# A decode block with its gradients on one core: attention by batch instead of by head group, and VectorE 32-bit transposes instead of TensorE transposes

## The chip, the core and the metric

The kernel runs on 1 core of one Trainium2 chip. The metric is the device time of one execution in microseconds (us). The kernel before took 311.61 us in the median of 3 runs (310.44 to 313.74). One further execution was recorded with the hardware profiler; every row of a profile below is from that one.

Engines: PE is TensorE (PEld its weight loads), DVE is VectorE, ACT is ScalarE, POOL is GpSimd, SP is SyncE. SP, ACT and POOL can each issue DMAs, each into a queue of its own (q1, q10 and q0 in the profile); the 16 DMA engines serve all three.

## The reference

One decode step of a block with attention and a feed-forward network (FFN) side by side, and the gradients of all its inputs:

```python
xn  = layernorm(x)                                   # x: [4, 1, 512], bf16
q   = xn @ wq                                        # 32 heads of 128
k,v = last 1024 of 4096 rows of the caches [4, 8, 4096, 128], each kv-head for 4 heads
p   = softmax(q k^T / sqrt(128));  o = p v
out = x + (o @ wo) + (gelu(xn @ w_gate) * (xn @ w_up)) @ w_down    # F = 1792
# and, for grad_out, the gradients of x, k_cache, v_cache, wq, wo, w_gate, w_up, w_down
```

The outputs are `out` and `dx` (tiny), `dk` and `dv` of the whole caches (33.6 MB each, of which the first 3072 of 4096 rows are zeros), `dwq` and `dwo` (4.2 MB each) and the three FFN weight gradients (1.8 MB each). So 81 MB are written and some 31 MB read. Each weight gradient is an outer product over only 4 batches. What takes work is that K, V and every weight are needed in two orientations, one as they lie in memory, and one transposed.

## The kernel before

**Stages.** Constants and the layer norm come first. Then comes the FFN, forward and backward. Then a loop over `t`, the NT = 4 groups of GP = 2 kv-heads (8 heads), each for all 4 batches: `pre` (query rows `qs` and `do` = the gradient that reaches each head's output, through `wo`), `masks`, `scores(t, 0)` (S, from K), `softmax`, `scores(t, 1)` (dP, from V), `softmax_d`, `odq` (rows of `o` and `dq`), `fin` (contributions to `out` and `dx`). The two sums over groups gather in `acc`; a chain of operations on rows finishes `out` and `dx` (lines 652 to 681).

**Transposes.** All are made by PE, as a matmul with the identity into a bf16 PSUM tile of 128x1024 that DVE copies out (`evac(..., half=True)`, line 92): K and V blocks `T_ps` (line 306), `wo` (258), `wq` (471), `w_down` (546), `w_gate` and `w_up` (619).

**Scores.** All four batches and eight heads of a group share one PSUM tile: 128 partitions are 4 quarters of the 1024 keys by 32 rows (batch, head). Four matmuls of 256 columns (line 311), one per quarter, use 32 columns of the array each, at different `tile_position`s.

**Gradient pieces.** A piece of `dv` or `dk` (line 406) is one matmul of 512 columns over 32 rows and one evacuation into a staging tile of 1 MB; eight pieces fill it, and POOL stores it. `dwo`, `dwq` and the FFN's weight gradients are made in pieces in the same way. Pieces aren't emitted where they are defined. They go to a list `bg`, and `tick(n)` emits the next n of them between other steps. `evac` gives each float32 evacuation to ACT or DVE by a running balance of estimated costs (lines 83 to 92).

**Order of issue.** Tile schedules the engines' instructions itself, except those of SP, which keep the written order. SP issues: the rows of `x` and `grad_out`, `w_gate`, `w_up`, `w_down`, `wo` and `wq` of group 0, K and V of group 0 (two tiles each), `wo` and `wq` of group 1, the first K and V tile of group 1, and then the zeros: 32 DMAs of 1.5 MB (line 233), each waiting for the one two before it. All later loads are issued by ACT: K and V (line 213) from rings of three tiles of 1 MB each, `wo` and `wq` (206, 208) of the group after next from rings of two. All results are stored by POOL (line 96), except the two small ones.

**Rows in memory.** A K or V tile has contiguous runs of 2 KB, `wo` and `w_down` runs of 1 KB, `wq` 2 KB, `w_gate` and `w_up` 3.5 KB, zeros 6 KB.

Of the kernel before, what the change touches and what calls it, by code (L numbers as in the profile page):

```python
# [13 lines left out]
BF16 = mybir.dt.bfloat16  # L14
P = 128
# [3 lines left out]
def kernel(  # L19
# [34 lines left out]
    ND = D // P  # L54
    NF = F // P
    J = W // P
    GP = 2
    NT = G // GP
    HG = GP * rep
    RG = B * HG  # L60
    NQ = P // RG
    WQ = W // NQ
    JQ = J // NQ
    NS = B * GP
    CW = HG * Dh
    assert Sq == 1 and Dh == P and D == 512 and F % P == 0 and RG == 32 and JQ * NQ == J and WQ == JQ * P
    scale = float(Dh) ** -0.5
    eps = 1e-5

    const = ctx.enter_context(tc.tile_pool(name="const", bufs=1))  # L70
    kvp = ctx.enter_context(tc.tile_pool(name="kvp", bufs=3))
    wres = ctx.enter_context(tc.tile_pool(name="wres", bufs=2))
    attw = ctx.enter_context(tc.tile_pool(name="attw", bufs=2))
    tsb = ctx.enter_context(tc.tile_pool(name="tsb", bufs=5))
    outp = ctx.enter_context(tc.tile_pool(name="outp", bufs=3))
    ps_w = ctx.enter_context(tc.tile_pool(name="ps_w", bufs=4, space=bass.MemoryType.PSUM))
    ps_a = ctx.enter_context(tc.tile_pool(name="ps_a", bufs=1, space=bass.MemoryType.PSUM))
    ps_x = ctx.enter_context(tc.tile_pool(name="ps_x", bufs=1, space=bass.MemoryType.PSUM))
# [4 lines left out]
    def evac(out, in_, n, half=False, eng=None):  # L83

        eng = "dve" if half else eng
        ca, cd = (190 + n) / 1.2, (120 + (n / 2 if half else n)) / 0.96
        if eng is None:
            eng = "act" if load["act"] + ca <= load["dve"] + cd else "dve"
        load[eng] += ca if eng == "act" else cd
        if eng == "act":  # L90
            return nc.scalar.copy(out=out, in_=in_)  # L91
        return nc.vector.tensor_copy(out=out, in_=in_)  # L92

# [7 lines left out]


    RB = P // B
    x_b = const.tile([P, D], BF16, name="x_b")
    dy_b = const.tile([P, D], BF16, name="dy_b")
    for dst, src in ((x_b, A_x), (dy_b, grad_out)):
        nc.sync.dma_start(out=dst[:], in_=bass.AP(tensor=src.tensor, offset=src.offset,
                                                  ap=[[D, B], [0, RB], [1, D]]))
# [8 lines left out]
    msk_i = const.tile([P, rep], FP32, name="msk_i")  # L117
    nc.vector.reduce_sum(out=msk_i[:], in_=ident_f[:].rearrange("p (b r) -> p r b", b=B)[:, 0:rep, :], axis=AX.X)


    rsum = const.tile([P, NQ, RG], FP32, name="rsum")
    nc.gpsimd.memset(rsum[:], 1.0)

    msk_f = const.tile([P, GP, B], FP32, name="msk_f")
    nc.gpsimd.memset(msk_f[:], 1.0)
    for q in range(NQ):
        rs = slice(q * RG, (q + 1) * RG)
        nc.gpsimd.affine_select(out=rsum[rs], in_=rsum[rs], pattern=[[0, NQ], [-1, RG]],
                                compare_op=ALU.is_equal, fill=0.0, base=0, channel_multiplier=1)
        nc.gpsimd.affine_select(out=msk_f[rs], in_=msk_f[rs], pattern=[[-rep, GP], [-HG, B]],  # L130
                                compare_op=ALU.is_ge, fill=0.0, base=0, channel_multiplier=1)
        nc.gpsimd.affine_select(out=msk_f[rs], in_=msk_f[rs], pattern=[[rep, GP], [HG, B]],
                                compare_op=ALU.is_ge, fill=0.0, base=rep - 1, channel_multiplier=-1)
    msk = const.tile([P, GP, B], BF16, name="msk")
    nc.vector.tensor_copy(out=msk[:], in_=msk_f[:])
# [4 lines left out]

    qm_all, dom_all = [], []
    for i in range(2):
        for lst, nm in ((qm_all, "qm"), (dom_all, "dom")):
            t_ = const.tile([P, NS, RG + rep], BF16, name=f"{nm}{i}")
            nc.gpsimd.memset(t_[:], 0.0)
            lst.append(t_)


    acc = const.tile([P, 2, ND, B], FP32, name="acc")
    nc.vector.memset(acc[:], 0.0)  # L150

    def acc_add(o, ps):
        nc.vector.tensor_tensor(out=acc[:, o], in0=ps, in1=acc[:, o], op=ALU.add)

    def acc_sum(o, terms):

        ps = ps_w.tile([P, ND, B], FP32, name="acc_ps", tag="w")
        for c in range(ND):
            for k, (lf, rhs) in enumerate(terms):
                nc.tensor.matmul(ps[:, c, :], lhsT=lf(c), rhs=rhs, start=(k == 0), stop=(k == len(terms) - 1))  # L160
        acc_add(o, ps[:])


    od_ps = ps_a.tile([P, 2, GP, Dh], FP32, name="od_ps")
    nc.vector.memset(od_ps[:], 0.0)
# [11 lines left out]
    xn_f = const.tile([P, D], FP32, name="xn_f")  # L177
    nc.vector.tensor_scalar(out=xn_f[:], in0=x_b[:], scalar1=mv[:, 0:1], scalar2=rstd[:, 0:1],
                            op0=ALU.subtract, op1=ALU.mult)
    xn_b = const.tile([P, D], BF16, name="xn_b")  # L180
    nc.vector.tensor_copy(out=xn_b[:], in_=xn_f[:])

    xnT = const.tile([P, ND, B], BF16, name="xnT")
    dyT = const.tile([P, ND, B], BF16, name="dyT")
    for src, dstT in ((dy_b, dyT), (xn_b, xnT)):
        tps = ps_x.tile([P, ND, P], BF16, name="tps", tag="x")
        for c in range(ND):
            nc.tensor.transpose(tps[:, c, :], src[:, c * P:(c + 1) * P], ident[:])
        nc.vector.tensor_copy(out=dstT[:], in_=tps[:].rearrange("p c (b r) -> p c b r", b=B)[:, :, :, 0])


    xnm = const.tile([P, rep, D], BF16, name="xnm")
    dym = const.tile([P, rep, D], BF16, name="dym")
    for src, dst in ((dy_b, dym), (xn_b, xnm)):
        for i in range(rep):
            nc.vector.tensor_scalar(out=dst[:, i, :], in0=src[:], scalar1=msk_i[:, i:i + 1], scalar2=None,
                                    op0=ALU.mult)


    wo_v = A_wo.rearrange("(t h p) n -> t p h n", p=P, h=HG)  # L200
    wq_v = A_wq.rearrange("(c p) (t j) -> t p c j", p=P, j=CW)
    wo_t, wq_t, k_t, v_t = {}, {}, {}, {}

    def load_w(t, eng):
        wo_t[t] = wres.tile([P, HG, D], BF16, name="wo_sb", tag="wo")
        eng.dma_start(out=wo_t[t][:], in_=wo_v[t])
        wq_t[t] = wres.tile([P, ND, CW], BF16, name="wq_sb", tag="wq")
        eng.dma_start(out=wq_t[t][:], in_=wq_v[t])  # L208

    def load_kv(t, k, g, eng):  # L210
        d_, src, nm = ((k_t, A_k_cache, "kb"), (v_t, A_v_cache, "vb"))[k]
        tl = kvp.tile([P, B, J, Dh], BF16, name=nm, tag=nm)
        eng.dma_start(out=tl[:].rearrange("p b j d -> p b (j d)"),  # L213
                      in_=src[:, t * GP + g, K0:Sk, :].rearrange("b (m j) d -> m b (j d)", j=J))
        d_[(t, g)] = tl

    def load_next(t, k):

        if t + 1 < NT:
            load_kv(t + 1, k, 1, nc.scalar)  # L220
        if t + 2 < NT:
            load_kv(t + 2, k, 0, nc.scalar)


    ZG = 2
    zlist = [(og, b, g) for b in range(B) for g in range(0, G, ZG) for og in (out_2, out_3)]

    def zeros():

        zsrc = bass.AP(tensor=ztile.tensor, offset=ztile.offset, ap=[list(ztile[:].ap[0]), [0, ZG], [1, ZW]])  # L230
        done = []
        for og, b, g in zlist:
# [8 lines left out]
    bg = deque()  # L241

    def tick(n):
        for _ in range(min(n, len(bg))):
            bg.popleft()()


    st = {}

    def pre(t):  # L250

        wo_sb, wq_sb = wo_t[t], wq_t[t]
        dq_ps = ps_x.tile([P, 2, HG, B], FP32, name="doq_ps", tag="x")
        for h2 in range(HG // 2):
            wT_ps = ps_w.tile([P, 2, ND, P], BF16, name="woT_ps", tag="w")
            for i in range(2):
                for c in range(ND):
                    nc.tensor.transpose(wT_ps[:, i, c, :], wo_sb[:, 2 * h2 + i, c * P:(c + 1) * P], ident[:])  # L258
            woT = tsb.tile([P, 2, ND, P], BF16, name="woT", tag="wT")
            evac(woT[:], wT_ps[:], 1024, half=True)  # L260
            for i in range(2):
                for c in range(ND):
                    nc.tensor.matmul(dq_ps[:, 0, 2 * h2 + i, :], lhsT=woT[:, i, c, :], rhs=dyT[:, c, :],
                                     start=(c == 0), stop=(c == ND - 1))
            tick(2)
        for h in range(HG):
            for c in range(ND):
                nc.tensor.matmul(dq_ps[:, 1, h, :], lhsT=wq_sb[:, c, h * Dh:(h + 1) * Dh], rhs=xnT[:, c, :],
                                 start=(c == 0), stop=(c == ND - 1))
# [27 lines left out]
    def scores(t, k):  # L297
# [4 lines left out]
        for g in range(GP):  # L302
            for b in range(B):
                T_ps = ps_w.tile([P, J, P], BF16, name="T_ps", tag="w")
                for j in range(J):
                    nc.tensor.transpose(T_ps[:, j, :], blks[(t, g)][:, b, j, :], ident[:])  # L306
# [405 lines left out]
```

## Time and profile before

| | |
|---|---|
| median of 3 runs | 311.61 us (310.44 to 313.74) |
| span of the profiled execution, first to last instruction | 311.7 us |
| bytes moved by DMA | 112.38 MB, 34405 packets |
| mean granted PE clock | 0.738 of full |
| busy: PE, DVE, ACT, POOL | 224.1, 146.3, 113.4, 51.3 us |
| queue q1 (SP) | 66.59 MB in 18136 packets |
| queue q0 (POOL) | 30.67 MB in 7808 packets |
| queue q10 (ACT) | 14.69 MB in 8432 packets |
| first and last zeros issued | 38.9 and 256.5 us |

The profile gives a span and no other time for its execution. The page cuts the span into 40 slices of 7.8 us; a digit there is the busy share in tenths. In the groups of instructions, the first two numbers behind the bar are the busy time of the group in us and the mean of one in ns; what follows the second bar is the idle time of that engine just before them, and what ended most of it. The chain of waits is followed back from the last instruction, at each step to whatever released it. ACTq, SPq and POOLq in it are those engines' sequencers issuing DMAs.

### The profile page before, as it was taken

To read this page: it belongs to the slowest core of one execution; us is meant where nothing else is said; L and a number is where in the kernel's file an instruction comes from. 1 tells how busy PE (TensorE), PEld (TensorE's weight loads), DVE (VectorE), ACT (ScalarE), POOL (GpSimd) and SP (SyncE) were. 2 spreads that over 40 slices of the span, in tenths; PEclk is the share of its full clock that TensorE was granted. 3 is DMA by queue.
4 is the path that set the end of the run, shared out by engine and by line. 5 is a ranking of instruction groups with operands and counts; after the bars stand their busy time and mean duration, and the time that the engine had idled before them with its cause. 6 is when DMAs were issued, how large, how long until landed. Compare 5 with 4: busy or idle time off the path is not lost.

```text
span 311.7 us, 6831 instructions
## 1 busy us (share of the span) xinstructions
PE 224.1 (72%) x2950; PEld 144.7 (46%) x2956; DVE 146.3 (47%) x304; ACT 113.4 (36%) x217; POOL 51.3 (16%) x76
## 2 busy tenths in 40 slices
PE   1269986936988379779648069969789755979861
PEld 0259874615555244465425044455556333756231
DVE  5246663523743234537414025546545424564766
ACT  3010645613613045346022044435244414533650
POOL 6000121610100005201000004201000501110140
PEclk9998998875975555779955555679955559895585
DMA  5999999999999999999999999998999999431494
GB/s 167 397 351 385 374 402 416 416 422 424 419 295 392 418 374 418 421 420 419 375 418 414 357 418 416 421 420 346 394 410 405 418 422 418 159 145 62 181 335 160
DMA packets 34405, 112.38 MB, mean 361 GB/s; under 512 B 1664, under 2 KB 7816, under 8 KB 34376
## 3 DMA queue, kind: packets, MB, share of 16 engines
q1 hardware_dynamic: 18136, 66.59, 53.6%
q0 software_dynamic: 7808, 30.67, 24.8%
q10 hardware_dynamic: 8432, 14.69, 13.6%
q8 instruction: 23, 0.38, 0.5%
q14 instruction: 6, 0.05, 0.0%
HBM read 30.93 MB, written 81.01 MB: 359 GB/s over the span
## 4 chain that ended last, share of the span: by engine, by line
PE 39%; DMA 30%; ACTq 9%; DVE 8%; issue 6%; ACT 4%; POOL 1%; SPq 1%; DVEq 0%; POOLq 0%
PE T_ps L306 11%; DMA kb<-in_A_k_cache_dram 10%; PE kv_ps L406 7%; ACTq L208 6%; DMA wd_sb<-in_B_w_down_dram 6%; DMA out_dram<-osb_o 5%; DMA vb<-in_A_v_cache_dram 5%; PE S_ps L311 4%; ACTq L213 3%; DMA out_dram<-osb_d 3%; DMA out_dram<-osb_g 2%; PE dwo_ps L426 2%; PE wgT_ps L619 2%; PE wdT_ps L546 2%; PE wqT_ps L471 2%
## 5 line engine op out<-in xcount | busy, mean ns | idle before, releaser
L92 DVE COPY T_sb<-T_ps 128x1024 bf16<-128x1024 bf16 x64 | 44.2, 691 | 41.5 <-PE T_ps L306 40.9
L91 ACT CAST stg_dk<-kv_ps 128x512 bf16<-128x512 f32 x46 | 25.0, 590 | 47.0 <-issue 26.9
L91 ACT CAST stg_dv<-kv_ps 128x512 bf16<-128x512 f32 x52 | 28.2, 590 | 31.9 <-PE kv_ps L406 22.7
L306 PE MATMUL T_ps<-ident,kb 128*128 128x128 bf16 x256 | 32.9, 280 | 6.1 <-DMA kb<-in_A_k_cache_dram 5.0
L406 PE MATMUL kv_ps<-qmr,dS_b 32*128 32x512 bf16 x64 | 23.1, 598 | 16.9 <-ACT stg_dk L91 16.4
L306 PEld LDWEIGHTS <-kb 128*128 128x128 bf16 x256 | 23.0, 125 | 22.2 <-issue 13.3
L306 PE MATMUL T_ps<-ident,vb 128*128 128x128 bf16 x256 | 26.6, 242 | 0.2
L406 PE MATMUL kv_ps<-domr,P_b 32*128 32x512 bf16 x64 | 18.6, 476 | 5.9 <-DVE wqT L92 3.0
L306 PEld LDWEIGHTS <-vb 128*128 128x128 bf16 x256 | 19.0, 109 | 8.0 <-issue 4.8
L91 ACT CAST osb_g<-dwg_ps 128x384 bf16<-128x384 f32 (+1 forms) x30 | 14.4, 534 | 17.2 <-DMA out_dram<-osb_g 5.9
L92 DVE COPY woT<-woT_ps 128x1024 bf16<-128x1024 bf16 x16 | 11.1, 691 | 20.2 <-PE woT_ps L258 20.2
L92 DVE CAST stg_dk<-kv_ps 128x512 bf16<-128x512 f32 x18 | 12.1, 686 | 16.8 <-PE kv_ps L406 16.6
L258 PEld LDWEIGHTS <-wo_sb 128*128 128x128 bf16 x128 | 11.4, 127 | 17.5 <-issue 17.2
L91 ACT CAST osb_o<-dwo_ps 128x512 bf16<-128x512 f32 x23 | 12.8, 587 | 17.1 <-PE dwo_ps L426 15.3
L91 ACT CAST osb_q<-dwq_ps 128x512 bf16<-128x512 f32 x25 | 13.6, 589 | 13.8 <-PE dwq_ps L441 9.2
L92 DVE COPY wqT<-wqT_ps 128x1024 bf16<-128x1024 bf16 x16 | 11.1, 691 | 15.7 <-PE wqT_ps L471 15.7
L96 POOL DMA_DIRECT2D out_dram<-stg_dv x8 | 6.0, 754 | 72.9 <-ACT stg_dv L91 41.8
L258 PE MATMUL woT_ps<-ident,wo_sb 128*128 128x128 bf16 x128 | 15.5, 285 | 1.3 <-DVE stg_dk L92 0.8
L471 PEld LDWEIGHTS <-wq_sb 128*128 128x128 bf16 x128 | 11.1, 129 | 10.5 <-issue 10.5
L471 PE MATMUL wqT_ps<-ident,wq_sb 128*128 128x128 bf16 x128 | 14.8, 287 | 0.8 <-DVE stg_dv L92 0.8
L96 POOL DMA_DIRECT2D out_dram<-stg_dk x8 | 6.1, 767 | 54.6 <-ACT stg_dk L91 42.5
L91 ACT CAST osb_d<-dwd_ps 128x512 bf16<-128x512 f32 x14 | 8.1, 586 | 14.3 <-PE dwd_ps L580 13.4
(182 smaller groups left out, 349.3 us busy)
## 6 DMA issues: line engine op xcount, KB each, us to landing
out_dram<-ztile SPq DMA_DIRECT2D x32, 1536.0 KB, 11.2
out_dram<-stg_dv POOLq DMA_DIRECT2D x8, 1024.0 KB, 11.5
out_dram<-stg_dk POOLq DMA_DIRECT2D x8, 1024.0 KB, 12.4
vb<-in_A_v_cache_dram ACTq DMA_DIRECT2D x5, 1024.0 KB, 15.8
kb<-in_A_k_cache_dram ACTq DMA_DIRECT2D x5, 1024.0 KB, 26.0
out_dram<-osb_o POOLq DMA_DIRECT2D x8, 512.0 KB, 10.4
out_dram<-osb_q POOLq DMA_DIRECT2D x8, 512.0 KB, 4.7
out_dram<-osb_g POOLq DMA_DIRECT2D x8, 448.0 KB, 7.4
```

Source lines behind the costliest of these rows:

```text
L91: return nc.scalar.copy(out=out, in_=in_)
L92: return nc.vector.tensor_copy(out=out, in_=in_)
L96: d = eng.dma_start(out=out, in_=in_)
L208: eng.dma_start(out=wq_t[t][:], in_=wq_v[t])
L213: eng.dma_start(out=tl[:].rearrange("p b j d -> p b (j d)"), in_=src[:, t * GP + g, K0:Sk, :].rearrange("b (m j) d -> m b (j d)", j=J))
L258: nc.tensor.transpose(wT_ps[:, i, c, :], wo_sb[:, 2 * h2 + i, c * P:(c + 1) * P], ident[:])
L306: nc.tensor.transpose(T_ps[:, j, :], blks[(t, g)][:, b, j, :], ident[:])
L311: nc.tensor.matmul(ps[q * RG:(q + 1) * RG, :], lhsT=lf[:, s * RG:(s + 1) * RG], rhs=T_sb[:, q * WQ:(q + 1) * WQ], start=(g == 0 and b == 0 ...
L406: nc.tensor.matmul(mps[:].rearrange("p b d -> p (b d)"), lhsT=src[rs, jj * P:(jj + 1) * P], rhs=mr[rs, g].rearrange("p b d -> p (b d)"), s ...
L426: nc.tensor.matmul(mps[:], lhsT=o_r[:, g, :], rhs=dym[:, i, :], start=True, stop=True)
L471: nc.tensor.transpose(wT_ps[:, i, c, :], wq_sb[:, c, h * Dh:(h + 1) * Dh], ident[:])
L546: nc.tensor.transpose(wT_ps[:, i, c, :], wd_sb[:, 2 * f2 + i, c * P:(c + 1) * P], ident[:])
```

## The change

The kernel is rewritten from the layer norm on; what is computed, the zeros and their pacing stay.

- **Loop.** Attention goes over the 4 batches, each with all 8 kv-heads (32 heads). Head vectors for all batches are made once ahead of it, and `dwo`, `dwq`, `out` and `dx` once after it. `bg` and `tick` go; pieces are emitted where they are defined.
- **Transposes.** DVE transposes blocks of 32x32 (`t32`). bf16 data are taken as pairs, 32 bits each (`pairs`), into a scratch tile of 128x1024 words (two of them), whose even or odd halves the matmuls read with a stride of two. The PE's transposes with their copies go.
- **Scores.** One matmul contracts over 128 partitions = 4 blocks of 32 keys by 32 word-rows of one head; so four of 256 columns are needed for each head, and their weights `bd` are mostly zeros, with the query's values refilled for each batch by four ACT copies.
- **Gradient pieces** of `dv` and `dk` contract over all 128 partitions, with `spread` holding the probabilities on block diagonals.
- **Queues.** SP loads `w_gate`, `w_up`, `w_down` in contiguous runs of 14 KB per partition, all of `wq` and `wo` in runs of 32 KB, K of batch 0, and then issues the zeros. POOL loads all other K and V (2 tiles of 1 MB, runs of 2 KB) and stores all results (staging tiles of 1 MB, three instead of four). ACT issues only the two small outputs. V has one buffer, K two.
- **FFN math** is done on 128 partitions x 448 (32 repeated rows by 14), where it was 128 x 56.

The core of the diff:

```diff
-    def evac(out, in_, n, half=False, eng=None):
+    def evac(out, in_, n):
+        ca, cd = (190 + n) / 1.2, (130 + n) / 0.96
+        eng = "act" if load["act"] + ca <= load["dve"] + cd else "dve"
...
+    def t32(out, in_, n):
+        load["dve"] += (60 + n) / 0.96
+        nc.vector.transpose(out=out, in_=in_)
+
+    def pairs(ap):
+        return ap.bitcast(U32)
+
+    def scratch():
+        return scrp.tile([P, 1024], U32, name="scr", tag="scr")
...
-        wg_sb = ffn_w.tile([P, ND, F], BF16, name="wg_sb")
-        nc.sync.dma_start(out=wg_sb[:], in_=B_w_gate.rearrange("(c p) f -> p c f", p=P))
...
+        nc.sync.dma_start(out=wg_sb[:].rearrange("p c f -> p (c f)"), in_=B_w_gate.rearrange("(p c) f -> p (c f)", c=C))
...
+        nc.sync.dma_start(out=wq_sb[:].rearrange("p c n -> p (c n)"), in_=A_wq.rearrange("(p c) n -> p (c n)", c=C))
+        nc.sync.dma_start(out=wo_sb[:].rearrange("p k n -> p (k n)"), in_=A_wo.rearrange("(p k) n -> p (k n)", k=KH))
+        load_kv(0, 0, kap, "ka", nc.sync)
+        zeros()
...
+    with tc.tile_pool(name="pre", bufs=1, reuse_waits="tile") as pre:
...
+        for npb in range(NPB):
+            sc = scratch()
+            t32(sc[:].rearrange("p (k n) -> p k n", k=KH), pairs(wo_sb[:])[:, :, npb * Q:(npb + 1) * Q], 1024)
+            sb = sc[:].bitcast(BF16).rearrange("p (u k r) -> p u r k", u=2, r=2)
+            for r in range(2):
+                for u in range(2):
+                    mm(do_ps[u][:].rearrange("p k n -> p (k n)"), dyBD[:, npb, r, :], sb[:, u, r, :],
+                       npb == 0 and r == 0, npb == NPB - 1 and r == 1)
...
+        def scores(k, b):
+            refill(k, b)
+            ps = bank("sc_ps", ("S", "dP")[k], (P, J * Q))
+            halves = (k_t, v_t)[k][b]
+            for g2 in range(G // 2):
+                sc = scratch()
+                t32(sc[:], pairs(halves[g2 // 2][:, (g2 % 2) * 2:(g2 % 2) * 2 + 2].rearrange("p g j d -> p (g j d)")), 1024)
+                sb = sc[:].bitcast(BF16).rearrange("p (g j e m r) -> p g e r j m", g=2, j=J, e=2, r=2)
+                for g in range(2):
+                    for e in range(2):
+                        for r in range(2):
+                            gg = 2 * g2 + g
+                            mm(ps[:].rearrange("p (j m) -> p j m", j=J),
+                               bd[k][:, gg, 2 * e + r].rearrange("p a g i -> p (a g i)"),
+                               sb[:, g, e, r], gg == 0 and e == 0 and r == 0, gg == G - 1 and e == 1 and r == 1)
+            return ps[:]
...
+        def transposed(src, k):
+            pT = att.tile([P, J, Q], BF16, name="pT", tag=f"pT{k}")
+            t32(pT[:], src[:].rearrange("p (j m) -> p j m", j=J), 256)
+            for q in quad:
+                nc.vector.tensor_copy(out=spread[k][q, :, q], in_=src[q].rearrange("p (j m) -> p j m", j=J))
+            return pT
...
+        def dvdk(k, b, rows):
+            mr = att.tile([P, G, Dh], BF16, name="mr", tag=f"mr{k}")
+            masked(mr[:], rows[:, b, :], G)
+            og = (out_3, out_2)[k]
+            for hf in range(2):
+                stg = stg_tile()
+                sv = stg[:].rearrange("p (g j d) -> p g j d", g=G2, j=J)
+                for j in range(J):
+                    ps = bank("kv_ps", "w", (P, G2, Dh))
+                    mm(ps[:].rearrange("p g d -> p (g d)"), spread[k][:, j, :],
+                       mr[:, hf * G2:(hf + 1) * G2, :].rearrange("p g d -> p (g d)"))
+                    evac(sv[:, :, j, :], ps[:], 512)
+                result(og[b, hf * G2:(hf + 1) * G2, K0:Sk, :].rearrange("g (m j) d -> m g (j d)", j=J),
+                       sv.rearrange("p g j d -> p g (j d)"))
...
+        for b in range(B):
+            S = scores(0, b)
+            dP = scores(1, b)
+            P_f, P_b = softmax(S)
+            pT = transposed(P_b, 0)
+            odq(0, b, pT)
+            if b + 1 < B:
+                load_kv(b + 1, 1, att, "va", nc.gpsimd)
+            dvdk(0, b, dr_b)
+            dS_b = softmax_d(P_f, dP)
+            dST = transposed(dS_b, 1)
+            odq(1, b, dST)
+            if b + 2 < B:
+                load_kv(b + 2, 0, (kap, att)[b % 2], ("ka", "kb")[b % 2], nc.gpsimd)
+            dvdk(1, b, qr_b)
```

After the loop the stage `fin` picks each head's rows of `o` and `dq` by masks (`heads`, two DVE operations on 128x1024 each), makes `dwo` in 32 pieces and `dwq` in 32 pieces, `out` by 32 matmuls of 512 columns with `wo`, the part of `dx` that comes through `wq` by 8 transposes of 1024 words and 128 matmuls of 128 columns, and ends with the chain of row operations on 4 partitions. In it, `masked` and `heads` run on DVE.

## The prediction

> **What bounds the kernel now.** I read the page's 40 slices first, to see which resource is full, and when.
>
> ```profile
> PEclk9998998875975555779955555679955559895585
> DMA  5999999999999999999999999998999999431494
> ...
> DMA packets 34405, 112.38 MB, mean 361 GB/s; under 512 B 1664, under 2 KB 7816, under 8 KB 34376
> ```
>
> The DMA engines are full up to slice 34 and mostly idle in the last six. Three stretches of the span (columns: length; PE, PEld, DVE, ACT and POOL busy; clock, DMA share, GB/s) put numbers on that.
>
> ```profile
> 0.00:45.00 45.00, 29.43 (x594) 25.71 (x595) 24.80 (x67) 12.82 (x21) 7.81 (x28) 0.96 0.97 344
> 45.00:265.00 220.00, 160.43 (x1955) 98.93 (x1959) 93.28 (x184) 79.87 (x158) 35.90 (x39) 0.70 1.02 404
> 265.00:312.00 47.00, 34.24 (x409) 20.01 (x407) 28.21 (x53) 20.67 (x38) 7.62 (x10) 0.72 0.46 172
> ```
>
> So there are two limits: bytes until 265 us, and then 47 us in which the last head group is computed beside idle queues. The chain of waits shows why that group is late: besides PE it holds loads, and ACT's own queue, where an ACT that issues a load can't evacuate.
>
> ```profile
> PE 39%; DMA 30%; ACTq 9%; DVE 8%; issue 6%; ACT 4%; POOL 1%; SPq 1%; DVEq 0%; POOLq 0%
> ```
>
> Next I read the DMA queues from 238 to 244 us, where all three are loaded (packets, MB, share).
>
> ```profile
> q1 hardware_dynamic: 211, 1.20, 47.9%
> q0 software_dynamic: 203, 0.83, 34.1%
> q10 hardware_dynamic: 214, 0.44, 18.9%
> ```
>
> The three queues get equal numbers of packets, so a queue's rate goes with its packet size: 5.7 KB for the zeros on q1 (SP), 4.1 KB for stores on q0 (POOL), 2.1 KB for loads on q10 (ACT). That is why a load of 1 MB takes two to three times as long as 1.5 MB of zeros:
>
> ```profile
> out_dram<-ztile SPq DMA_DIRECT2D x32, 1536.0 KB, 11.2
> kb<-in_A_k_cache_dram ACTq DMA_DIRECT2D x5, 1024.0 KB, 26.0
> wo_sb<-in_A_wo_dram ACTq DMA_DIRECT2D x2, 1024.0 KB, 36.3
> ```
>
> Last come the groups of instructions that the change removes or moves. The first is the evacuation of transposes; the second shows ACT idle for 26.9 us behind its own issues.
>
> ```profile
> L92 DVE COPY T_sb<-T_ps 128x1024 bf16<-128x1024 bf16 x64 | 44.2, 691 | 41.5 <-PE T_ps L306 40.9
> L91 ACT CAST stg_dk<-kv_ps 128x512 bf16<-128x512 f32 x46 | 25.0, 590 | 47.0 <-issue 26.9
> L306 PE MATMUL T_ps<-ident,kb 128*128 128x128 bf16 x256 | 32.9, 280 | 6.1 <-DMA kb<-in_A_k_cache_dram 5.0
> ```
>
> The sum is made against this execution's span of 311.7 us. The median of the three runs is 311.61, so nothing is added.
>
> **Bytes.** The tensors are the same, so the 112.4 MB stay, 50.3 of them zeros in 32 DMAs, still two at a time behind 16 MB of loads on SP. Weights get longer rows; I price that at 0 (at best 16 MB at 404 instead of 344 GB/s, -7 us; at worst nothing, since start-up and K rows are in that mean). For full DMA I take 0.41 MB/us, between 0.404 here and the 0.42 of 253 to 265 us.
>
> **Loads move from ACT to POOL.** 14 loads of 1 MB (14.7 MB of K and V) now queue on q0 among the stores. ACTq's 9% of the chain, 28 us, goes. POOL gets 14 issues of 0.77 us (its issues take 0.754 to 0.786), 11 us on an engine 16% busy: 0 on the path, and 0.8 us per load if POOL were full. The new wait: POOL stops at each V load until the outputs' matmuls have read the only V buffer. Queued behind it are the dv stores, and the evacuations wait for those once three staging tiles are full. That is what is late next. The Trainium skill ("DMA: Bandwidth & Descriptors", SWDGE vs HWDGE vs iDMA) speaks against this move: POOL writes its descriptors into SBUF, from which VectorE's two-port modes lock it out. It gives no price, and no row here shows such a wait; by the rule the sum could only grow.
>
> For K/V loads on q0 I take the 4.1 KB packets of the dk/dv stores, which have the same rows. Beside zeros of 5.7 KB, q0 then gets 42%: 0.172 MB/us, and zeros 0.238. The bounds are q10's 2.1 KB (0.11 MB/us; zeros then end at 221, V waits in each batch, about 300 in all) and an even split (0.205).
>
> **Transposes.** Out go 936 PE transposes (106 us of PE over seven groups) and 117 DVE copies of 691 ns, 80.8 us. In come 77 VectorE transposes, 66,240 32-bit elements per partition. The trace has none. Below them lies the plain fp32 copy of 1024 elements (`acc_r`, 683 ns). One element per cycle follows from fp32 reductions of 256 and 512 elements (419 and 681 ns, so 1.02 ns each): 1.21 us for 1024. For the upper end I double that slope, 2.25. I take 1.21, since every fp32 row but the plain copies lies on that line: 68 + 77 x 0.16 = 80 us. DVE gains nothing; PE does. The Trainium skill ("Vector Engine (DVE) Microarchitecture Reference", section 3.8) states one element per cycle per lane for transposes, at its 0.96 GHz an estimated 1.07 us plus start; by it the sum is as here.
>
> **TensorE.** Scores keep 256 matmuls of 256 columns, but four no longer share the array, and dv/dk (128 of 512) lose the same overlap. A 512-column matmul costs 0.43 us at clock 0.57 (eight in 3.45 us at 295.7) and half that at full clock. A batch has 49k columns: 21 to 41 us, 28 at the mean clock of 0.74. The batch's DMA time below hides it.
>
> **Small edits.** Masks go from POOL (8 x 1.89) to DVE (8 x 1.21 = 10 us); 32 ACT copies of 0.28 refill the score weights, 9 us. Both lie in a batch's DMA time: 5 us per batch if that cover is gone.
>
> **Front.** FFN math runs on 448 columns instead of 56. DVE until attention: elementwise 11 us, 16 transposes 16, copies and masks 6, some 20 evacuations 14, `wo` transposes 9.7, rest of the head vectors 4. That is 61 us after the first weight at 11: 72, where the first scores now come at 52. V of batch 0 is asked for only then, as its memory is the FFN's, and lands 2.1/0.172 = 12 us later. Zeros use the DMA meanwhile.
>
> **Body.** From 45 to 72 us 11.1 MB move: 5.5 of FFN results, 5.6 of zeros. After that q0 has 31.5 MB of attention (14.7 in, 16.8 out), 183 us: 255. The other 44.7 MB of zeros end at 260. That is 46 us per batch, above its compute: scores 11, softmax 5 (68.7 to 73.5 us in before), outputs 2 x 4.5, dv with the second softmax step 9.3 (16 evacuations of 590 ns on ACT, since the balance charges DVE for transposes), dk 6, together 41 in series. Compute runs 1.5 MB, 9 us, ahead of the last store and ends at 246.
>
> **End.** On DVE: half of 64 evacuations 22, head picks 4.8, masks 3.6, `wq` transposes 9.7, copies 1.8, together 42; then the row chain and a landing, 8 (now from 304.9); less 5 beneath the last dk: 45. Beside it lie ACT 20, PE 37 (66k columns at 0.74) and 20 us of stores. 246 + 45 = 291, and 4 for hand-overs between engines: **295 us**, 16.7 below now.
>
> **Rivals.** *Bytes only* (faster still): the end's work moves ahead under the zeros. 45 + (112.4 - 15.5)/0.41 + 3 = 284, at 0.42 279: 282. For it speaks the DMA full for 220 us; against it, that the end needs the last batch's outputs.
>
> *Steps in series* (slower): if engines keep program order, a batch is 41.6: 72 + 8 for V + 166 = 246, and two waits of 8 for staging tiles that q0 hasn't drained, 262. The end in series is 25.6 (64 pieces) + 9.6 (out_0) + 11 (last transposes) + 8 + 9 (head picks) = 63: 325. For it: before's last group takes 59 us after its K lands (252.7). Against: PE ran line 607 at 2.6 us and scores at 239.05 amid the next group's vectors, so work does move ahead. It decides once body and end lose 17 us together.
>
> *Slow transposes* (slower): at 2.25 us the front grows by 24 us, the end by 9, the batches by some 8, of which the zeros' head start returns 16: 320. It decides at about 1.9 us.
>
> **How the numbers follow.** Chances: forecast 0.47, bytes only 0.13, series 0.25, slow transposes 0.15. The forecast's own range is 286 to 309, from q0's share and the clock at the end. The range of 277 to 332 takes in the rivals and leaves out under 2 in 10. Within 1% (308.5 to 314.7, about what can't be told from no change) lie 0.03 of the forecast and 0.02 of each slow rival. Faster: 0.44 + 0.13 = 0.57; same 0.07; slower 0.36.
>
> **What will show it.** Right: ACTq gone from the chain; equal packets on q0 and q1, q0 at 42% of their bytes; zeros over near 260; transposes of 1024 at 1.2 us; last attention evacuation near 246; then under 50 us with DVE the fullest. Wrong: zeros over before 230 with idle DMA after (series); transposes above 1.9; q0 packets of 2 KB in loads; DMA full to the last 5 us (bytes only).

## The result and the profile after

The changed kernel takes 350.87 us (median of 4 runs, 349.74 to 353.09), the kernel before 312.68 on the same chip: a ratio of 1.122 [1.114, 1.130]. The forecast was 295. The profiled execution has a span of 348.0 us, 53.0 above the forecast, and all lines below are of it. First the 40 slices of 8.7 us:

```profile
PEclk9999766995856996888778589876589755555587
DMA  7999999999999999999999999998404702355600
...
DMA packets 20975, 112.15 MB, mean 322 GB/s; under 512 B 1368, under 2 KB 1632, under 8 KB 19296
```

The bytes are the same. The DMA engines are full up to slice 28, as before up to 34, but after that come twelve slices, in most of which they are idle for 40% of the time or more, where before there were six. Seven of those twelve stand at a clock of 0.5, six of them in a row. Three stretches of the span (columns as in the prediction: length; PE, PEld, DVE, ACT and POOL busy; clock, DMA share, GB/s) are the batches beside the zeros, the rest of the last batch, and the end:

```profile
80.00:243.00 163.00, 102.80 (x469) 52.81 (x470) 62.51 (x106) 62.63 (x137) 25.17 (x26) 0.77 1.01 403
243.00:275.00 32.00, 21.94 (x73) 7.40 (x72) 15.27 (x31) 18.07 (x35) 3.95 (x6) 0.82 0.40 157
275.00:348.00 73.00, 53.48 (x242) 17.86 (x242) 44.77 (x68) 20.33 (x37) 11.82 (x18) 0.57 0.32 130
```

The forecast had attention computed by 246 and 45 us after it. The last evacuation of attention is at 272.7, and 75.4 follow: 26.7 and 30.4 too much, less the 4 us of hand-overs, are the 53.0 but for rounding.

**Before 272.7.** From 120 to 130 us the two queues share by packets as forecast, 442 against 440, and q0 (loads and stores of attention) gets 1.69 of 4.21 MB, 40% (forecast: 42):

```profile
q1 hardware_dynamic: 442, 2.52, 60.4%
q0 software_dynamic: 440, 1.69, 41.4%
```

What this does to the loads stands in the DMA rows (KB each, median us from issue to landing). A store lands in 5.2 us, a load that shares its queue with stores in 21 to 32:

```profile
out_dram<-ztile SPq DMA_DIRECT2D x32, 1536.0 KB, 12.4
out_dram<-stg POOLq DMA_DIRECT2D x24, 1024.0 KB, 5.2
...
va<-in_A_v_cache_dram POOLq DMA_DIRECT2D x8, 1024.0 KB, 21.1
...
kb<-in_A_k_cache_dram POOLq DMA_DIRECT2D x4, 1024.0 KB, 32.1
```

q0 was not always loaded, though. Its row from 72 to 82, from 102 to 112 and from 252 to 262 us:

```profile
q0 software_dynamic: 1, 0.00, 0.2%
...
q0 software_dynamic: 118, 0.42, 10.3%
...
q0 software_dynamic: 88, 0.29, 7.8%
```

Between 112 and 242 us it moved 1.3 to 2.1 MB in every 10 us (forecast: 1.7), so the middle batches go at about the pace of its share. In these three stretches it had next to nothing to move: ahead of the first V load (asked for at 77.6), while the only V buffer was still being read (the second V load is asked for at 111.0), and after the last load had landed. Against 1.7 MB in 10 us some 4.4 MB are missing there, about 26 us of q0's share: an estimate from these rows, in the last of which the zeros were already over.

V of the last batch is asked for at 199 and 201 and lands at 232 and 238. VectorE's row in time (start, length, operation; in brackets its idle time and what ended it) shows what stands behind it:

```profile
232.56 2.37 DVE L93 STREAM_TRANSPOSE scr<-va 128x1024 uint32<-128x1024 uint32 x2 [3.22 <-DMA va<-in_A_v_cache_dram]
234.85 0.23 DVE L456 TENSOR_REDUCE mx<-mT_ps 1x32 f32<-1x128 f32 x1
...
238.74 2.37 DVE L93 STREAM_TRANSPOSE scr<-va 128x1024 uint32<-128x1024 uint32 x2 [3.40 <-DMA va<-in_A_v_cache_dram]
241.04 0.12 DVE L463 COPY negm<-nm_ps 128x1 f32<-128x1 f32 x1
...
248.06 0.16 DVE L470 RECIPROCAL rr<-es_ps 128x1 f32<-128x1 f32 x1
```

The maximum and its sign (`mx`, `negm`) need only K's scores, yet they stand behind V's transposes in VectorE's order, and the reciprocal stands behind evacuations. So the softmax and all that follows, two outputs, dv and dk, begins after V has landed, and this takes 34 us. A transpose of 1024 takes 1.23 us (1.21 forecast), and all 77 together take 82.2 us (80 forecast):

```profile
L93 DVE STREAM_TRANSPOSE scr<-va 128x1024 uint32<-128x1024 uint32 x16 | 19.2, 1229 | 32.3 <-DMA va<-in_A_v_cache_dram 21.1
```

**After 272.7.** The chain of waits holds only this part, and no DMA:

```profile
PE 13%; DVE 4%; POOL 1%; issue 1%; ACT 1%; DVEq 0%
```

The end falls into four stretches: head picks and masks; dwo, dwq and the output matmuls (`ob_ps`); the input gradient's matmuls; its row chain.

```profile
275.00:283.00 8.00, 1.19 (x5) 0.48 (x6) 6.38 (x7) 0.00 (x0) 7.47 (x10) 0.50 0.34 131
283.00:324.50 41.50, 40.58 (x100) 7.42 (x101) 22.62 (x32) 19.74 (x36) 3.82 (x7) 0.50 0.38 157
324.50:340.00 15.50, 10.79 (x133) 9.48 (x134) 11.32 (x17) 0.58 (x1) 0.53 (x1) 0.74 0.30 124
340.00:348.00 8.00, 0.93 (x8) 0.49 (x6) 4.45 (x12) 0.00 (x0) 0.00 (x0) 0.68 0.00 1
```

In the second TensorE is busy for 40.6 of 41.5 us, at a clock of 0.50 throughout, while VectorE and ScalarE have half their time free.

### The profile page after: what moved, and what is told of

Same layout as the page of the kernel before. It is cut to its first block, busy times and chain, and to the rows that moved or that the text cites. A ratio compares the mean times of both kernels' runs of the same rounds, so it can differ in the third digit from the quotient of the medians.

```text
span 348.0 us, 3250 instructions
## 1 busy us (share of the span) xinstructions
PE 230.3 (66%) x1179; PEld 103.3 (30%) x1179; DVE 183.4 (53%) x302; ACT 127.1 (37%) x259; POOL 53.9 (15%) x73
## 5 line engine op out<-in xcount | busy, mean ns | idle before, releaser
L88 ACT CAST stg<-kv_ps 128x512 bf16<-128x512 f32 x108 | 56.8, 599 | 48.1 <-PE kv_ps L117 25.9
L117 PE MATMUL sc_ps<-scr,bd 128*128 128x256 bf16 x256 | 50.1, 333 | 36.5 <-DVE scr L93 21.5
L117 PE MATMUL kv_ps<-mr,spr 128*128 128x512 bf16 x128 | 49.1, 439 | 20.3 <-ACT stg L88 15.8
L106 POOL DMA_DIRECT2D out_dram<-stg x30 | 19.8, 660 | 214.1 <-ACT stg L88 117.7
L117 PEld LDWEIGHTS <-bd 128*128 128x128 bf16 x256 | 29.4, 117 | 65.4 <-issue 46.2
L93 DVE STREAM_TRANSPOSE scr<-va 128x1024 uint32<-128x1024 uint32 x16 | 19.2, 1229 | 32.3 <-DMA va<-in_A_v_cache_dram 21.1
L117 PE MATMUL od_ps<-va,pT 128*32 128x512 bf16 x64 | 22.2, 524 | 3.7 <-DVE pT L93 3.7
L89 DVE CAST stg<-kv_ps 128x512 bf16<-128x512 f32 x20 | 13.3, 686 | 17.8 <-PE kv_ps L117 10.4
L117 PEld LDWEIGHTS <-spr 128*128 128x128 bf16 x128 | 13.7, 110 | 29.2 <-issue 22.2
L117 PE MATMUL ob_ps<-wo_sb,oK 128*4 128x512 bf16 x32 | 16.7, 606 | 0.0
L117 PE MATMUL dwo_ps<-dy_b,oSP 32*128 32x512 bf16 x32 | 15.3, 618 | 0.0
## 6 DMA issues: line engine op xcount, KB each, us to landing
va<-in_A_v_cache_dram POOLq DMA_DIRECT2D x8, 1024.0 KB, 21.1
```

Source lines behind the costliest of these rows:

```text
L93: nc.vector.transpose(out=out, in_=in_)
L106: d = eng.dma_start(out=out, in_=in_)
L117: nc.tensor.matmul(out, lhsT=lhsT, rhs=rhs, start=first, stop=last, **kw)
```

## The experiments

All times are medians of four runs, except for experiment 8, which ran once. The kernel before took 315.1 to 316.3 us in the median beside them, and 312.68 beside the changed kernel, which was not run again; so a difference of 3 us to its 350.87 says little. "Attention ends" means the last evacuation of dk in the one profiled execution.

**1. Without the zeros** (they are left out of the two cache gradients). Edit: `- zeros()`.

> Edit: the zeros of the two cache gradients aren't written (that part of the outputs is left out; 50 of 112 MB). Theory (the zeros keep the V loads and the stores of attention late): V of the last batch lands before 205 us instead of 239, attention's last evacuation is at 235 to 245 instead of 272.6, the end stays at 73 to 76 us: 310 to 322. Rival (the batches are a chain of steps on the engines, whatever the DMA does): attention ends at 265 or later and the time is above 340.

291.01 us. Attention ends at 215.8, far earlier than the theory had it; what is left, 75.4, is as long as in the changed kernel. From V's first transpose at 91.6 the four batches take 31 us each. The 57 us that attention lasts longer in the changed kernel come with the zeros.

**2. Zeros in shorter runs**: the same bytes, packets of 2 KB.

```
- ZG = 2
+ ZG = 1
  ...                     # the source in pieces of 1024 elements
- og[b, g:g + ZG, 0:K0, :].rearrange("g (m j) d -> m g (j d)", m=P)
+ og[b, g, 0:K0, :].rearrange("(c m j) d -> m c (j d)", m=P, j=8)
- if len(done) >= 2:      # the wait for done[-2]
+ if len(done) >= 4:      # the wait for done[-4]
```

> Edit: zeros in runs of 2 KB instead of 6 KB, same bytes, 64 DMAs of 768 KB with four under way instead of 32 of 1.5 MB with two. Theory (queues share by packets, so the loads' queue gains when the zeros' packets shrink): q0 gets 60 to 70% of the bytes in the body instead of 40%, V of the last batch lands by 220 us, attention ends 15 to 27 us earlier and the zeros later, at 275 to 300, beneath the end: 324 to 338. Rival (the share is not what makes V late, or the smaller packets cost bandwidth): 345 or more.

299.08 us, ratio 0.941 [0.931, 0.951] to the kernel before, far below the theory's range: the run length (with DMAs of half the size and as many bytes under way) takes 52 us off. Its queues from 120 to 130 us, again with equal packets:

```profile
q0 software_dynamic: 710, 2.72, 66.7%
q1 hardware_dynamic: 707, 1.38, 36.6%
```

q0 now has 66% of the bytes, V loads land in 13.3 instead of 21.1 us (median), and attention ends at 217.9, nearly as early as without zeros. The zeros lie beneath the end, which takes 80.6 us, and the DMA is full to slice 38:

```profile
DMA  6999999999999999999999999998999999999930
```

**3. Loads on ScalarE's queue**, as in the kernel before. Edit: `nc.gpsimd` to `nc.scalar` in the batches' four `load_kv` calls.

> Edit: the K and V loads of the batches are issued by ScalarE instead of GpSimd; undoes that part of the change. Theory (one shared queue's share is what makes V late): loads no longer stand behind stores, three queues with packets of 4.1, 4.1 and 5.7 KB give attention about 58% of the bytes instead of 40%, V of the last batch lands by 220 us, attention ends at 245 to 260: 322 to 338. Rival (ScalarE, stopped at each load for the V buffer, loses in evacuations what the queue gains): 345 to 360.

342.76 us, 8 below the changed kernel, between what the theory and the rival gave. A third queue helps far less than the packets of the zeros. In its profiled execution, the longest of the four (348.40), attention ends at 271.5 against 272.7, although V's last transposes begin at 229.3, 9.4 earlier than there: `mx` follows only at 243.4 in VectorE's order, behind eight evacuations and two transposes of `wq`. What the shorter executions gained was not traced.

**4. Softmax ahead of the dP scores.**

```
  S = scores(0, b)
- dP = scores(1, b)
  P_f, P_b = softmax(S)
  pT = transposed(P_b, 0)
+ dP = scores(1, b)
```

> Edit: in each batch the softmax and its transposes are emitted before the dP scores, so the small vector steps stand ahead of the V transposes in VectorE's queue. Theory (order within an engine's queue holds up the softmax while V is waited for): in the last batch the exponential runs as soon as the K scores are there, not after V has landed; 8 to 9 us go from the wait after V in the last batch, and since a V buffer comes free sooner, some 2 to 4 us per earlier batch: 333 to 344. Rival (only the landing of V matters): 348 to 353.

343.17 us: 7.7 less, at the upper edge of the theory's range, and attention ends at 266.1, 6.6 earlier. The last batch's exponential runs at 226.4, ahead of V's landing, instead of 241.3. So the order in VectorE's queue does cost time, but less than the theory's 8 to 9 us in the last batch and 2 to 4 in each earlier one.

**5. Masks built early**, after the first batch, in a pool of their own. **6. Only the pool**: 6.25 KB of unused memory in the same place, the masks left where they were.

```
+ late = ctx.enter_context(tc.tile_pool(name="late", bufs=1, reuse_waits="tile"))
+ gap = late.tile([P, 3200], BF16, name="gap")   # 5: selb, selh, dqs, perm
  with tc.tile_pool(name="att", bufs=1, reuse_waits="tile") as att:
```

> Edit: the masks selb and selh, the zeroed dqs and perm are built by GpSimd after the first batch, not at the head of the end. Theory: the chain of waits begins with them, about 5 us of GpSimd before the first head pick's matmul, so the time falls by 4 to 6 us: 345 to 347. Rival (another step of the end is due at that moment, above all VectorE's head pick, 1.9 us per reduction): less than 2 us, 349 to 351.

> Edit: the changed kernel with 6.25 KB per partition of unused memory ahead of the batches' memory, so that V's first buffer no longer lies on what the head vectors use; masks stay where they were. Theory (the early start of the first V load, 61 instead of 78 us, and not the masks, gave most of the 24 us of the kernel with the early masks): attention ends at 257 to 262 and the time is 332 to 340, or 326 to 332 where the clock at the end happens to rise. Rival (the masks gave it): 346 to 353.

326.93 us, below both ranges, and 329.66, as the theory of the pool had it. My theory of the masks falls: from attention's end to the first `ob_ps` matmul are 10.6 us in the changed kernel and with the pool alone, and 8.8 with early masks, so these are worth 1.8. What both kernels share is that V's first buffer no longer lies on memory the head vectors use: its load is issued at 59 to 61 instead of 77.6, and attention ends at 259.2 and 259.5, 13 earlier. The rest is the clock at the end. The four runs of 6 are pairs, 321.6 and 323.2 at a mean clock of 0.80, and 336.2 and 339.9 at 0.76. The profiled one is of the shorter pair, and its dwo and dwq stretches show it:

```profile
270.00:285.00 15.00, 15.00 (x54) 3.87 (x53) 11.81 (x17) 9.77 (x19) 1.70 (x3) 0.89 0.40 164
285.00:297.00 12.00, 11.05 (x45) 2.91 (x44) 9.86 (x16) 9.24 (x18) 2.13 (x4) 0.87 0.79 326
```

The same instructions take 27 us here and 41.5 in the changed kernel.

**7. dwo and dwq over 128 rows**, 96 of them zero.

```
+ for a in range(NQ):    # bm[:, a] is 1 in row group a
+     nc.vector.tensor_scalar(out=dyq[:, a, :], in0=dy_b[:], scalar1=bm[:, a:a + 1], scalar2=None, op0=ALU.mult)
+     ...                # xnq from xn_b likewise
- mm(ps[:], oSP[q, k, :], dy_b[q, :], pos=(Q * a, 0))
+ mm(ps[:], oSP[:, k, :], dyq[:, a, :])
  ...                    # dwq likewise
```

> Edit: the 64 matmuls of dwo and dwq contract over all 128 rows instead of 32 (the other 96 rows of one operand are masked to zero); columns and number of matmuls stay as they are. Theory (the clock follows the rows in use): the clock of 0.50 at 283 to 320 us rises to 0.8 or more, the 512-column matmuls of these groups fall from about 0.43 us apart to 0.25 or less, and the time from the last attention evacuation to the end falls by 12 to 18 us: 333 to 339. Rival (the end is bound by evacuations on VectorE and ScalarE, as my forecast had it, or by the four-column output matmuls that stand between them): clock and time stay, 347 to 353.

338.85 us, 12.0 less. The stretch of dwo and dwq, with as many columns and matmuls as before, takes 26 us instead of 41.5; making the masked operands probably costs some 3 us of this, since the first `ob_ps` matmul comes 13.8 us after attention's end instead of 10.6 (the profiled execution is the longest of the four, 342.28):

```profile
292.00:318.00 26.00, 25.43 (x93) 7.46 (x92) 20.00 (x31) 19.06 (x35) 3.83 (x7) 0.97 0.60 248
```

**8. The clock by itself**: sections of 60 matmuls of 512 columns, nothing else computed. A row group is a quarter of the 128 rows that a matmul can contract over.

> Leaves out the whole computation: seven sections of 60 matmuls of 512 columns each, with TensorE idle for about 9 us between them, over 32 rows, over 128 rows with a 4-column stationary, the mix of the two that the end of the changed kernel has, over 64 rows, over 128 rows, over 32 rows in row groups that take turns, and over 128 rows of which 96 hold zeros. Theory (the clock follows the rows in use): 0.50 and 0.43 us a matmul all through the sections over 32 rows, 1.00 and 0.215 us after the first 4 to 7 us over 128 rows; the section of 128 rows by 4 columns decides whether columns count too, the one with zeros whether data does. Rival (any busy TensorE rises within 4 to 7 us): every section reaches 1.00.

The sections' windows, in this order: 32 rows; 128 rows by 4 columns; the mix; 64 rows; 128 rows; 32 rows in turning row groups; 96 of 128 rows zero. The clock column tells nothing for the first two of these, since the trace has no clock event ahead of 46.7 us.

```profile
5.00:31.50 26.50, 25.64 (x60) 8.72 (x60) 0.35 (x1) 0.00 (x0) 1.00 0.01 5
43.50:58.00 14.50, 14.50 (x60) 5.27 (x58) 0.04 (x1) 0.00 (x0) 1.00 0.01 1
69.40:99.50 30.10, 29.66 (x60) 4.12 (x60) 0.68 (x3) 0.00 (x0) 0.50 0.00 0
110.40:137.00 26.60, 25.78 (x60) 8.71 (x60) 1.06 (x3) 0.00 (x0) 0.50 0.00 1
148.50:163.50 15.00, 15.00 (x60) 6.25 (x60) 0.24 (x1) 0.00 (x0) 0.87 0.00 0
175.00:185.00 10.00, 9.57 (x60) 2.94 (x60) 0.62 (x3) 0.00 (x0) 0.50 0.01 2
196.50:211.50 15.00, 14.98 (x60) 6.24 (x60) 0.29 (x1) 0.00 (x0) 0.87 0.00 0
```

From their starts, matmuls over 32 and over 64 rows are 0.43 us apart to the last one. Those over 128 rows are 0.43 apart at first and 0.22 from 3.5 to 4.1 us on, 0.25 on average, with 4 columns, 128 columns or zeros. In this execution TensorE being busy alone doesn't raise the clock; a contraction over 128 rows does (whether it is fewer rows that keep it down or the row groups that go with them is not told apart here). In turns the 32-row matmuls are 0.15 us apart on average at clock 0.50: the row groups overlap.

**9. Row groups in turn** in dwo and dwq.

```
- for a, q in enumerate(quad):
-     for u in range(2):
+ for u in range(2):
+     for a, q in enumerate(quad):
  ...                    # dwo likewise, staged by k pairs, stores of 2 KB runs
```

> Edit: dwo and dwq keep their 32 rows, but successive matmuls take the four row groups in turn instead of eight times the same one (dwo's stores become runs of 2 KB). The rows in use at a time stay few. Theory (matmuls of different row groups overlap, as the section with turns showed: 0.16 us apart at clock 0.50): the clock stays 0.50, the 64 matmuls stop being the limit, evacuations at 0.32 us a piece are it, and dwo and dwq take 24 to 27 us instead of 38.6: 334 to 341. Rival (only the clock helps): 347 to 353.

339.12 us, 11.8 less, for the most part by overlap instead of clock:

```profile
285.00:314.00 29.00, 27.46 (x95) 5.76 (x94) 20.08 (x32) 18.81 (x34) 4.53 (x7) 0.62 0.59 230
```

The 0.62 comes from the clock's late rise: it is 0.50 up to 304.9.

**10. Input gradient first**: the end's `dq_r`, dxq matmuls and row chain written ahead of dwo, dwq and `ob`; the lines are only moved.

> Edit: in the end, the input-gradient chain (dq_r, its 128 dxq matmuls, the row chain and its store) is written ahead of dwo, dwq and the output matmuls; nothing else changes. Theory (the end is a chain of steps in their written order; the 23 us after the last dwq evacuation could lie beside the evacuations): matmuls fill the end instead, some 41 us at half clock and 11 for dxq, then a store: 335 to 343. Rival (VectorE's 42 us of work, or the matmuls alone, are the length in any order): 347 to 353.

333.25 us, 17.6 less and a little below the theory's range. TensorE is full from 285 to 315, now also with the dxq matmuls that followed alone before:

```profile
285.00:295.00 10.00, 10.00 (x73) 5.64 (x72) 5.59 (x9) 3.22 (x6) 0.00 (x0) 0.63 0.01 2
295.00:305.00 10.00, 9.90 (x98) 5.65 (x95) 7.30 (x14) 6.18 (x13) 1.17 (x2) 1.00 0.27 107
305.00:315.00 10.00, 9.51 (x38) 2.44 (x37) 8.02 (x14) 4.66 (x10) 1.07 (x2) 1.00 0.60 249
```

Part of the gain is the clock, which rose with these 128-row matmuls; the order alone is not separated from it.

**11. Softmax order, pool, 128 rows and input gradient first together**, zeros as they are.

> Edit: the changed kernel with its zeros as they are (6 KB, two at a time), but the softmax ahead of the dP scores, dwo and dwq over 128 rows, the first V buffer moved off the head vectors' memory, and the input-gradient chain first in the end. Theory (these causes add up; single: 8, 12, 13 without the luck of the clock, 8 to 15): attention ends at 250 to 256, the end takes 50 to 56: 301 to 314. Rival (they overlap, the zeros' share keeps V late whatever else is mended): 318 to 330.

313.41 us: ratio 0.989 [0.980, 0.999], at the upper end of the theory's range. Attention ends at 255.1, and 56.6 follow. The single gains (7.7, 13, 12.0, 17.6) would sum to 50; together they give 37.5. A likely reason, not shown, is that two of them share the clock.

**12. A combined kernel**: 2, 4, 5 and 7 (the masked operands made by ScalarE).

> Edit: zeros in runs of 2 KB, softmax ahead of the dP scores, dwo and dwq over 128 rows (masked operands made by ScalarE) and masks built early. Theory (with attention done by 215 us the bytes are the limit and the rest of the end fits beneath them): the DMA engines are full to about 280 us at 0.38 to 0.41 MB/us, 112.2 MB, and the last rows follow within 8 us: 285 to 292. Rival (the end stays on the path, as in the first kernel with 2 KB runs): 295 to 300.

297.53 us, 0.947 [0.934, 0.961], in the rival's range. Attention ends at 205.5, yet ScalarE then stands for 20 us at the issue of the store of `out_0`, by the profile until a DMA of zeros is over:

```profile
ACT stg L88 <- DMA out_dram<-ztile: 20.3, 1, 20.3
```

**13. The row outputs stored by GpSimd instead.**

> Edit: the combined kernel, with the two small row outputs stored by GpSimd instead of ScalarE. There ScalarE stood 20.3 us at the issue of the first of them, until a DMA of zeros was over, with dwq evacuations behind it. Theory (that issue alone held the end): the 20 us go, dwq ends by 250 us, the last rows by 275, and the zeros are the last to end, at about 286: 287 to 292. Rival (the stores of dwo and dwq wait for their share beside the zeros as long): 294 to 299.

298.60 us: the theory of the issue falls as to the time. The wait is gone and the input gradient is done by 274, but the zeros end no sooner: their last DMA is issued at 287.6, in 12 at 283.0. The bytes were the limit either way.

**14. Runs of 2 KB only beside the batches**, 6 KB for the first 6 and last 24 DMAs of zeros.

```
+ n = 1024 if 6 <= len(done) < 40 else ZW
```

> Edit: as the one with the stores by GpSimd, but only the 34 DMAs of zeros that run beside the batches have runs of 2 KB, the first 6 and the last 24 have 6 KB. Theory (packets of 2 KB cost rate, 0.38 to 0.40 MB/us against 0.42): what is left after attention moves at 0.41 to 0.42 and the zeros end 3 to 6 us sooner: 281 to 288. Rival (the rate goes with reads and writes together, not with the runs; or the end's stores get so little beside 6 KB that the rows end last): 288 to 296.

292.87 us, 0.933 [0.923, 0.943]: the fastest kernel of this study that writes everything, though in the rival's range. The rate is part of it: from 209 to 274 us it moves 399 GB/s, the kernel of 13 moves 385. Its DMA is full almost throughout:

```profile
DMA  6999999999999999999999999969998999999992
```

**15. The kernel before with zeros in runs of 2 KB.**

> Edit: the kernel before, with zeros in runs of 2 KB, 768 KB a DMA and four under way. Its loads come in packets of 2.1 KB on ScalarE's queue. Theory (the share of the loads' queue is what the kernel before waits for as well, 30% of its chain is DMA): loads land in some 15 us instead of 26 to 36, the last head group starts earlier, and the zeros lie beneath its end: 290 to 303. Rival (the kernel before is held by its transposes on TensorE and its copies, or loses rate with 2 KB): 308 to 320.

299.79 us, 0.949 [0.942, 0.955], not to be told from the changed kernel with this edit (299.08): with the zeros' packets mended in both, no gain or loss of the rewrite is left that is clear of the noise. In the profiled execution, the longest of the four (305.11), K loads land in 14.4 us instead of 26.0 and the ScalarE loads of `wo` in 16.5 instead of 36.3; V loads, which landed in 15.8, gain little:

```profile
out_dram<-ztile SPq DMA_DIRECT2D x64, 768.0 KB, 13.0
...
vb<-in_A_v_cache_dram ACTq DMA_DIRECT2D x5, 1024.0 KB, 14.7
kb<-in_A_k_cache_dram ACTq DMA_DIRECT2D x5, 1024.0 KB, 14.4
```

## Why the prediction was wrong

- **Right.** Bytes, transposes (1.23 us against 1.21), equal packets on q0 and q1 and the share (40% against 42). The zeros ended at 247 instead of 260. ACTq is gone from the chain, but that chain covers only the end, and the 28 us set down for it never showed: with the loads back on ACT the kernel is 8 us faster (3).
- **"V of batch 0 ... lands 12 later".** It was asked for at 77.6, where the memory came free, not at the 72 I had; off that memory it is asked for at 59 to 61, and attention ends 13 earlier (5, 6). I took the FFN's memory for the only reason; the head vectors' pool lay there too.
- **"Compute runs 1.5 MB, 9 us, ahead of the last store, ends at 246": the step that failed.** I took a batch as the longer of its DMA time (46) and its compute (41). With one V buffer and the softmax written behind V's scores they in part follow one another: the load is asked for late, waits among stores, q0 runs empty meanwhile, and the last V still has its whole batch behind it, 34 us (238.7 to 272.7), so attention ended 26.7 later than the 246. The order was worth 6.6 (4), memory 13 (6), both 17.6 (11). Compute was in fact shorter than I had it: 31 us per batch where V comes at once (1). From V's first transpose at 90.7 the four batches take 45.5 each; that this is so near my 46 is luck in part, since it holds stretches of an empty q0 that I had not.
- **The share was right, its meaning wrong.** I used 42% for the time of the last byte on q0. It is above all how late the loads are, on which all else waits: at 66% attention ends 55 us sooner (2), more than all other edits of the batches together. My bound for it (0.205 MB/us, an even split) was in the text, and what it would do was never worked out.
- **"End ... together 42" on VectorE: the second step that failed**, 30.4 us of the 53. VectorE's 44.8 us were well sized, but did not set the length. Matmuls did: I priced 66k columns at a mean clock of 0.74, 37 us, and they ran at 0.50 for the most part, 53.5 us, and in series, head picks, dwo, dwq, dxq, rows. The 0.43 us for 512 columns that I read beside a clock of 0.57 mixed two clocks: in the kernel before it was 0.50 up to 298.6 us. Rows in use at 32 cost 12 (7, 9) to 16 (the pairs of 6), the written order up to 17.6 (10). With both mended, 56.6 remain (11), of which 10.6 are head picks and masks up to the first `ob_ps` matmul, where I had let 5 us of the end lie beneath dk.
- **The rivals.** "Steps in series" (325) was the nearest: its attention end was 262 and its end 63, and both were still longer, so 350.87 lies above everything that the forecast took in. Half of its sign was there, an idle DMA after the zeros, but these were over at 247, not before 230. Slow transposes and bytes only did not come. A chance of 0.25 for it was too low against a forecast that needed overlap in every batch and in the end.

The Trainium skill ("TensorE: Matmul & The Clock Gate", Part 1) says that some 3.4 us of sustained activity give TensorE its full clock. The end of the changed kernel differs, with 41 us busy at 0.50, and experiment 8 shows what counts besides: rows. That page's rule holds for the sections over 128 rows, where the clock rose after 3.5 to 4.1 us.

Why the clock rises under the same mix of 32-row and 4-column matmuls in some executions (6) and not in others, the traces answer in part. In all of them the clock changes only at steps of 3.41 us, which lie differently in each trace. The stretch of dwo opens with six or seven `ob_ps` matmuls over 128 rows, one after another, 2.7 to 3.1 us in all, at a clock of 0.50. In the changed kernel they begin at 283.27, so that a step ends amid them, at 284.92; in 6 they begin at 270.13 and fill one step up to 273.40. The steps that hold them and the ones after, first in the changed kernel, then in 6:

```profile
281.50:284.92 3.42, 1.98 (x6) 0.60 (x7) 2.67 (x5) 0.43 (x2) 0.97 (x2) 0.50 0.00 0
284.92:288.33 3.41, 3.41 (x9) 0.71 (x7) 2.19 (x3) 1.17 (x2) 0.00 (x0) 0.50 0.00 0
...
269.98:273.40 3.42, 3.42 (x10) 0.88 (x9) 2.36 (x2) 0.43 (x2) 0.00 (x0) 0.50 0.00 0
273.40:276.81 3.41, 3.41 (x14) 0.91 (x13) 2.52 (x4) 2.82 (x5) 0.00 (x0) 1.00 0.00 0
```

Of the eight traces with dwo over 32 rows, the clock rose right after this opening in the three where at least 2.6 us of it lay in one step (2, 5, 6), and not in the five where at most 2.1 us did (the changed kernel, 1, 3, 4, 9). So the 16 us between the pairs of 6 are probably luck of position. No run moved the opening on purpose, so this is a pattern and not shown as the cause; what makes the clock fall again within the mix stays open.

## What to carry to other kernels

Where queues share by packets, a bulk stream's packet size decides how late the loads beside it are; one run length in the zeros was worth 52 us, more than any other edit here, and 16 in the kernel before. Ask of each load what stands behind it in its engine's order and what memory it waits for: "hidden beside DMA" holds only if the next load is asked for before the compute that it would hide. In a tail of matmuls, count rows: contract over 128, or let the row groups take turns.

## What the runs showed of the hardware

- TensorE did not speed up in 25 us of matmuls over 32 or over 64 rows (0.43 us per 512 columns to the end, clock 0.50 in the latter), and did after 3.5 to 4.1 us over 128 rows, even with 4 columns or with 96 rows zero (8).
- The clock changes only at steps of 3.41 us, whose place differs between executions.
- 32-row matmuls of four row groups in turn overlap: 0.15 us apart on average at clock 0.50, against 0.43 in one row group.
- VectorE transposes 1024 32-bit elements per partition in 1.23 us.
- Packets of 2 KB cost some rate: 385 against 399 GB/s from 209 to 274 us in 13 and 14, one execution each.
